# Attention and expert kernel on one core: two softmax sums, a key transpose, half the exponentials and one quarter of a transposed tile are issued at other places

## Chip, cores and metric

One Trainium2 chip, one core. The time is the device time of one execution in microseconds (us); where several runs are given, their median counts. All kernels compute the same function on the same inputs in float32.

## The reference

Three stages follow each other. `B, H, S, D = 4, 8, 512, 64`, and each of the 32 (batch, head) pairs has 32 global tokens as well.

```
s_g   = q_g @ [k_g, k_l]^T / 8           # 32 x 544, softmax, times [v_g, v_l]
s_ll  = q_l @ k_l^T / 8, masked to |i-j| <= 32
s_l   = [q_l @ k_g^T / 8, s_ll]          # softmax, times [v_g, v_l]
x     = both outputs, as 2176 used rows x 512
g     = leaky_relu(x @ w_in)             # 512 -> 2048
x     = g @ w_out                        # 2048 -> 512
out   = soft mixture of 8 experts, 4 slots each, on x (phi, w1, w2)
```

The softmax is `e / (sum(e) + 1e-9)` with the row's maximum subtracted.

## The kernel before

Local attention goes by pairs of heads. A pair is `(b, i)`, batch 0 to 3 and pair 0 to 3. For each pair the kernel has these items, and the letters are used from here on:

- **T** (`a_T`, L383): keys and queries are transposed on TensorE, four 128x128 transposes each, into a PSUM bank of the tag `tp`. ScalarE copies each out (L394, tiles `kT` and `qT`); VectorE then copies the keys' windows (L405, L406). `kT` has 4 buffers, one for each pair of a batch. T ends by issuing the loads of a later pair on SyncE's queue.
- **S** (`a_S`, L418): 64 matmuls of scores for two heads into the two banks of the tag `sc`; VectorE adds the mask and takes maxima (L446), and ScalarE makes four exponentials for each head, each with a sum (L454). VectorE then adds 1e-9 to the sums and inverts them (L459, L460).
- **E** (`a_E`, L465): the exponentials of both heads are transposed, four transposes for each head, into two `tp` banks; VectorE copies them out (L477, tile `eT`).
- **V** (`a_V`, L481): 64 matmuls with the values into the bank `po`; VectorE multiplies by the inverted sums (L501).

Each batch has global attention too: **gS** (`g_S`, L508: scores `gl` in `sc` banks, `gg` in `tp` banks, maxima, exponentials, sums and their inverse), **gE** (`g_E`, L555: two transposed heads in `tp` banks), **gG** (`g_G`: two small transposes in `tp` banks), **gV**, **gX**.

The feed-forward stage goes by 17 row tiles t of 128 rows: **X t** (`b_X`, L667: four transposes into a `tp` bank, copied out by ScalarE at L680 and then read again by VectorE at L681), **H t fq a/b** (`b_H`, L692: twelve 512-column products for quarter q in two halves of six, then a leaky ReLU on ScalarE, L717, called the Prelu), **L q t** (`b_L`, L742: quarter q of tile t transposed into a `tp` bank and copied out), **M**, **D1**, **D2**, **D3** and **U t** (`b_M`, `b_D1`, `b_D2`, `b_D3`, `b_U`: the routing logits and the running column softmax).

The tag `tp` has two PSUM banks in all, for T, E, X, L, gS, gE, gG and gX together. `hb` (for H) has two.

What sets the order: for batches 2 and 3 attention items (`step`, L640) and feed-forward items (`b_items`, L992) are merged by `merge` (L1011) in proportion to hand-written weights, and TensorE runs them in exactly that order (`manual_schedule`). The order on the other engines comes from the framework's planner, which goes by the order of the program, by what is ready in its own timeline, and by edges given with `issue_after`: an instruction in such a block stands behind the named one on its own engine. During batch 2 the row tiles 4 to 7 are worked on, during batch 3 the tiles 7 to 10.

Of the kernel before, what the change touches and what calls it, by code (L numbers as in the profile page):

```python
# [13 lines left out]
AF = mybir.ActivationFunctionType  # L14
# [6 lines left out]
def kernel(  # L21
# [393 lines left out]
    def softmax_small(mx, nmx):  # L415
        nc.vector.tensor_scalar_mul(nmx, mx, -1.0)

    def a_S(b, i):  # L418
        qt, kw = qT.pop((b, i)), kwin.pop((b, i))
        mx = sa.tile([P, 2, NT], F32, tag="mx", name="mx", bufs=2)  # L420
        nmx = sa.tile([P, 2, NT], F32, tag="nmx", name="nmx", bufs=2)
        sm = sa.tile([P, NT, 2], F32, tag="sm", name="sm", bufs=2)
        rs = sa.tile([P, NT, 2], F32, tag="rs", name="rs", bufs=2)
        es = []
        bks = [bank("sc", f"sc{e}", 2) for e in range(2)]
        if b == 0:
            for bk in bks:
                warm(bk)
        seq_ = [(T, u, e) for T in range(NT) for u in range(4) for e in range(2)]
        for T, u, e in seq_ if b > 1 else sorted(seq_, key=lambda x: x[2]):  # L430
            U = 4 * T + u
            if True:
                if True:
                    last_a[0] = nc.tensor.matmul(  # L434
                        bks[e][32 * u:32 * u + 32, P * T:P * T + P],
                        qt[64 * e:64 * e + 64, 32 * U:32 * U + 32],
                        kw[win(U) // (NW // 2)][64 * e:64 * e + 64, win(U) % (NW // 2), :],
                        start=True, stop=True,
                    ).ins
        for e in range(2):  # L440
            bk = bks[e]
            s = sa.tile([P, S + SG], F32, tag="se", name="se", bufs=4)[:, 0:S].rearrange(
                "p (t k) -> p t k", t=NT
            )
            for T in range(NT):
                nc.vector.tensor_tensor_reduce(  # L446
                    out=s[:, T, :], in0=bk[:, P * T:P * T + P],
                    in1=mask[:, 0 if T == 0 else 2 if T == NT - 1 else 1, :],
                    scale=1.0, scalar=-3.0e38, op0=ALU.add, op1=ALU.max,
                    accum_out=mx[:, e, T:T + 1],  # L450
                )
            nc.vector.tensor_scalar_mul(nmx[:, e], mx[:, e], -1.0)  # L452
            for T in range(NT):
                exp_last[0] = nc.scalar.activation(  # L454
                    out=s[:, T, :], in_=s[:, T, :], func=AF.Exp,
                    bias=nmx[:, e, T:T + 1], accum_out=sm[:, T, e:e + 1],
                ).ins
            es.append(s)
        nc.vector.tensor_scalar_add(sm, sm, 1e-9)  # L459
        nc.vector.reciprocal(rs, sm)  # L460
        sc[b, i] = (es, rs)

    eT = {}

    def a_E(b, i):  # L465
        es, rs = sc[b, i]
        ets = []
        for e in range(2):
            pt = tp("etp")
            if b == 0:  # L470
                warm(pt)
            for T in range(NT):
                last_a[0] = nc.tensor.transpose(  # L473
                    pt[:, P * T:P * T + P], es[e][:, T, :], ident
                ).ins
            et = sa.tile([P, S], F32, tag="eT", name="eT", bufs=2)
            (nc.vector.tensor_copy if b or e else nc.scalar.copy)(et, pt)  # L477
            ets.append(et)
        eT[b, i] = ets

    def a_V(b, i):  # L481
        ets = eT.pop((b, i))
        _, rs = sc.pop((b, i))
        vw = vwin.pop((b, i))
        po = bank("po", "po", 1)
        if b == 0:
            warm(po)
        pov = po.rearrange("p (t e d) -> p t e d", t=NT, e=2)
        for T in range(NT):
            for e in range(2):  # L490
                for u in range(4):
                    U = 4 * T + u
                    last_a[0] = nc.tensor.matmul(  # L493
                        pov[32 * u:32 * u + 32, T, e, :],
                        ets[e][:, 32 * U:32 * U + 32],
                        vw[:, win(U), e, :],
                        start=True, stop=True,
                    ).ins
        if i == 0:
            xn[b] = (xb[0] if b % 2 else xa).tile([P, NT, H, D], F32, tag="xn", name="xn", bufs=1)  # L500
        nc.vector.tensor_tensor(  # L501
            out=xn[b][:, :, 2 * i:2 * i + 2, :], in0=pov,
            in1=rs.unsqueeze(3).to_broadcast([P, NT, 2, D]), op=ALU.mult,
        )
# [3 lines left out]
    def g_S(b):  # L508
        mx = sa.tile([P, 2, 2], F32, tag="gmx", name="gmx", bufs=1)
        nmx = sa.tile([P, 2], F32, tag="gnmx", name="gnmx", bufs=1)  # L510
        sm = sa.tile([P, 2, 2], F32, tag="gsm", name="gsm", bufs=1)
        rs = sa.tile([P, 2], F32, tag="grs", name="grs", bufs=1)
        es = []
        for e in range(2):
            bl = bank("sc", "gl", 2)
            bg = tp("gg")
            for i in range(NP):
                lq = qgT[64 * e:64 * e + 64, i, 32 * b:32 * b + 32]
                nc.tensor.matmul(
                    bl[32 * i:32 * i + 32, :], lq, kT[b, i][64 * e:64 * e + 64, :],  # L520
                    start=True, stop=True,
                )
            for i in range(NP):
                lq = qgT[64 * e:64 * e + 64, i, 32 * b:32 * b + 32]
                nc.tensor.matmul(
                    bg[32 * i:32 * i + 32, 0:SG], lq,
                    kgT[64 * e:64 * e + 64, i, 32 * b:32 * b + 32],
                    start=True, stop=True,
                )
            nc.vector.reduce_max(out=mx[:, e, 0:1], in_=bl, axis=AX.X)  # L530
            nc.vector.reduce_max(out=mx[:, e, 1:2], in_=bg[:, 0:SG], axis=AX.X)
            nc.vector.tensor_reduce(
                out=nmx[:, e:e + 1], in_=mx[:, e], axis=AX.X, op=ALU.max, negate=True
            )
            s = sa.tile([P, S + SG], F32, tag="se", name="gs", bufs=4)
            nc.scalar.activation(
                out=s[:, 0:S].rearrange("p (t q) -> p t q", t=NT),
                in_=bl.rearrange("p (q t) -> p t q", t=NT),
                func=AF.Exp, bias=nmx[:, e:e + 1],
                accum_out=sm[:, e, 0:1],  # L540
            )
            nc.scalar.activation(  # L542
                out=s[:, S:S + SG], in_=bg[:, 0:SG], func=AF.Exp, bias=nmx[:, e:e + 1],
                accum_out=sm[:, e, 1:2],
            )
            es.append(s)
        sms = sa.tile([P, 2], F32, tag="gsms", name="gsms", bufs=1)
        nc.vector.tensor_reduce(out=sms, in_=sm, axis=AX.X, op=ALU.add)
        nc.vector.tensor_scalar_add(sms, sms, 1e-9)
        nc.vector.reciprocal(rs, sms)  # L550
        for i in range(NP):
            kT.pop((b, i))
        gst[b] = [es, rs]

    def g_E(b):  # L555
        es, rs = gst[b]
        ets = []
        for e in range(2):
# [1 line left out]
            for T in range(NT):  # L560
                nc.tensor.transpose(pt[:, P * T:P * T + P], es[e][:, P * T:P * T + P], ident)
            et = sa.tile([P, S], F32, tag="eT", name="get", bufs=2)
            nc.vector.tensor_copy(et, pt)
            ets.append([et])
            if b < 2:
                g_G(b, e, ets)
        gst[b].append(ets)

    def g_G(b, e, ets):
        es = gst[b][0]  # L570
# [64 lines left out]
    def T_(n):  # L635
        a_T(*order[n])
        if n >= NP:
            load_ahead(n + 2)

    def step(n):  # L640
# [3 lines left out]
        e = (0.9, lambda: a_E(b, i))  # L644
        v = (1.6, lambda: (a_V(b, i), None if n < NP else load_vn(b) if i == NP - 2 else load_v(n + (1 if last else 2))))
        ns = [(2.7, lambda: a_S(*order[n + 1]))] if n + 1 < NN else []
        nt = [(0.9, lambda: T_(n + 2))] if n + 2 < NN else []
        if not last:
            gs = [(2.2, lambda: g_S(b))] if i == NP - 2 else []
            return ns + [e] + gs + nt + [v]  # L650
        gv = (2.1, lambda: (g_V(b), load_v(n + 2) if b else None))
        if b < 2:
            return [e, (0, lambda: None), v, (1.1, lambda: g_E(b))] + ns + nt + [gv]
# [38 lines left out]
    def b_H(t, f, half=None):  # L692
# [21 lines left out]
            return  # L714
        gs = gt[t][:, 512 * f:512 * f + 512]
        with ahead(t):
            nc.scalar.activation(out=gs, in_=hp, func=AF.Prelu, alpha=0.01)  # L717
        if t in BLK or t in HALF and f < 2:
            blocks(t, f, gs)

# [200 lines left out]
    def l_items(t):  # L921
        return ([(0.0, lambda: None), (0.6, lambda: b_M(t, range(2)))] if t in BLK else [
            (0.6, lambda: b_M(t, range(2))) if t in HALF else (0.9, lambda: (b_L(t, 0), b_L(t, 1))),
            (0.9, lambda: (b_L(t, 2), b_L(t, 3))),
        ]) + [
            (1.3, lambda: b_D1(t)),
            (0.3, lambda: first(b_D2, t)),
# [64 lines left out]
    def b_items(t0, t1):  # L992
        its, d3, u = [], [], []
        for t in range(t0, t1):
# [6 lines left out]
            if t - 1 in BLK:  # L1001
# [1 line left out]
                its += [li[3]] + h[5:8] + [li[4]]  # L1003
                d3, u = [], [li[5]]
                continue
            its += [h[0]] + d3 + [h[1]] + u + [li[1], h[2], h[3], li[0]] + x + [h[4], li[2]]
            its += [h[5], li[3], h[6], h[7]]
            d3, u = [li[4]], [li[5]]
        return its + d3 + u
# [424 lines left out]
```

## Time and profile before

| | |
|---|---|
| median of 3 runs | 492.76 us (491.17 to 493.52) |
| the profiled execution | 490.33 us, of which span 488.6 us |
| TensorE busy (matmul) | 451.3 us, 92% of the span |
| VectorE, ScalarE, GpSimd busy | 275.7, 234.2, 160.0 us (56, 48, 33%) |
| batches 2 and 3 | about 186 to 326 us from the span's start |
| mean granted TensorE clock | 0.970 of full speed |

The span runs from the first to the last instruction in the profile; 1.73 us of the profiled execution lie outside it. A matmul counts as busy from its start to a modelled end, so that the records of consecutive matmuls overlap.

### The profile page before, as it was taken

How to read it: one execution, taken by the hardware profiler on the slowest of the kernel's cores; microseconds unless marked ns; L12 is line 12 of the kernel's file. 1: busy time of each engine (PE TensorE's matmuls, PEld its weight loads, DVE VectorE, ACT ScalarE, POOL GpSimd, SP SyncE). 2: the span in 40 equal slices, each digit the busy share in tenths (PEclk: the TensorE clock that was granted, in tenths of full speed). 3: DMA queues.
4: the chain of work that ended last, by engine and by line, in shares of the span. 5: the costliest groups of instructions: out<-in, count | busy, mean ns of one | idle time of the engine just before them, and what ended most of it. 6: DMA issues, size and time to landing. Idle time of an engine off the chain costs nothing.

```text
span 488.6 us, 13462 instructions
## 1 busy us (share of the span) xinstructions
PE 451.3 (92%) x5341; PEld 316.7 (65%) x5341; DVE 275.7 (56%) x880; ACT 234.2 (48%) x678; POOL 160.0 (33%) x281
## 2 busy tenths in 40 slices
PE   7868789998989999999999998999999999999982
PEld 5645668676766666776777775777777777743341
DVE  4685879389557676566555655535665532242223
ACT  4776799587854445444245544134443342321021
POOL 2044887433310202632335160524775530000000
PEclk9985699999999999999999999999999999999997
DMA  9989688499664575442440230279200269989997
GB/s 177 224 201 248 203 246 346 149 310 303 204 167 109 115 150 88 102 104 62 130 107 1 60 60 19 71 259 405 112 1 2 87 224 318 395 324 397 349 304 253
DMA packets 111990, 90.23 MB, mean 185 GB/s; under 512 B 75256, under 2 KB 94392, under 8 KB 111928
## 3 DMA queue, kind: packets, MB, share of 16 engines
q1 hardware_dynamic: 110024, 88.33, 61.9%
q10 hardware_dynamic: 1904, 1.05, 0.8%
q8 instruction: 42, 0.69, 0.6%
q14 instruction: 20, 0.16, 0.1%
HBM read 76.68 MB, written 8.65 MB: 175 GB/s over the span
## 4 chain that ended last, share of the span: by engine, by line
PE 74%; ACT 7%; DMA 6%; DVE 5%; SPq 4%; issue 2%; POOL 1%; DVEq 0%; ACTq 0%; POOLq 0%
PE hp L709 37%; DMA rraw<-in_moe_w_in_dram 4%; PE gtp L747 3%; PE sc L434 3%; PE ehp L1298 3%; PE up L832 3%; PE po L493 2%; PE lg L761 2%; PE etp L473 2%; PE xtp L674 1%; PE wotp L345 1%; PE sop L1332 1%; SPq L162 1%; PE gpo L585 1%; ACT se L454 1%
## 5 line engine op out<-in xcount | busy, mean ns | idle before, releaser
L709 PE MATMUL hp<-wi,xxh 128*128 128x512 f32 x512 | 168.0, 409 | 1.3 <-ACT xxh L680 1.3
L738 POOL COPY g<-gb 32x256 f32<-32x256 f32 x206 | 82.6, 401 | 87.6 <-DVE gb L729 59.1
L709 PEld LDWEIGHTS hp<-wi,xxh 128*128 128x128 f32 x512 | 92.1, 191 | 24.2 <-issue 5.3
L709 PE MATMUL hp<-wi,xxl 128*128 128x512 f32 x256 | 101.5, 397 | 0.0
L717 ACT ACTIVATE g<-hp 128x512 f32<-128x512 f32 x60 | 35.7, 594 | 78.4 <-PE hp L709 70.0
L454 ACT ACTIVATE se<-se,nmx 128x128 f32<-128x128 f32 x128 | 49.7, 390 | 19.9 <-DVE nmx L452 17.2
L709 PEld LDWEIGHTS hp<-wi,xxl 128*128 128x128 f32 x256 | 48.6, 190 | 11.7 <-issue 0.8
L200 POOL COPY vw<-vw 32x1664 f32<-32x1664 f32 x10 | 15.8, 1579 | 72.1 <-DMA vw<-in_v_g_dram 29.7
L446 DVE CUSTOM_DVE_ANT_0 se<-sc,mask 128x128 f32<-128x128 f32 x128 | 28.9, 285 | 11.8 <-PE sc L434 11.7
L261 POOL TENSOR_TENSOR wn<-wn,rraw 128x512 int32<-128x512 int32 x16 | 22.7, 1424 | 35.6 <-DVE wn L257 33.4
L729 DVE STREAM_TRANSPOSE gb<-g 128x512 f32<-128x512 f32 x32 | 22.7, 709 | 19.8 <-ACT g L717 19.6
L434 PE MATMUL sc<-kw,qT 64*32 64x128 f32 x1024 | 27.5, 283 | 0.7 <-DVE mx L446 0.4
L261 POOL TENSOR_TENSOR wo<-wo,rraw 128x512 int32<-128x512 int32 x12 | 16.0, 1332 | 31.6 <-DVE wo L257 7.2
L493 PE MATMUL po<-vw,eT 128*32 128x64 f32 x1024 | 21.9, 229 | 3.4 <-issue 2.7
L434 PEld LDWEIGHTS sc<-kw,qT 64*32 64x32 f32 x1024 | 19.7, 109 | 7.6 <-issue 4.2
L454 ACT ACTIVATION_READ_ACCUMULATOR se<-se,nmx 128x1 f32 x128 | 24.1, 189 | 0.0
L493 PEld LDWEIGHTS po<-vw,eT 128*32 128x32 f32 x1024 | 17.4, 115 | 9.4 <-issue 8.0
L473 PE MATMUL etp<-identr,se 128*128 128x128 f32 x128 | 22.5, 300 | 0.2
L477 DVE COPY eT<-etp 128x512 f32<-128x512 f32 x28 | 18.4, 682 | 6.6 <-PE etp L473 6.6
L405 DVE COPY kw<-kT 128x672 f32<-128x672 f32 x32 | 20.0, 660 | 3.6 <-ACT kT L394 3.2
L747 PE MATMUL gtp<-identr,g 128*128 128x128 f32 x112 | 16.9, 281 | 4.7 <-ACT gs L542 1.9
L251 ACT ACTIVATE rraw<-rraw 128x512 int32<-128x512 uint32 x28 | 18.8, 674 | 4.7 <-POOL wo L261 2.8
(228 smaller groups left out, 757.2 us busy)
## 6 DMA issues: line engine op xcount, KB each, us to landing
ew<-in_moe_w_dram SPq DMA_DIRECT2D x23, 1024.0 KB, 8.8
rraw<-in_moe_w_in_dram SPq DMA_DIRECT2D x16, 512.0 KB, 6.2
ew<-in_moe_w_dram SPq DMA_DIRECT2D x15, 512.0 KB, 8.9
vw<-in_v_l_dram SPq DMA_DIRECT2D x60, 112.0 KB, 3.6
rraw<-in_moe_w_out_dram SPq DMA_DIRECT2D x12, 512.0 KB, 6.5
wo_f<-wo SPq DMA_DIRECT2D x16, 256.0 KB, 4.1
vn<-in_v_l_dram SPq DMA_DIRECT2D x4, 1024.0 KB, 6.0
wo<-wo_f SPq DMA_DIRECT2D x4, 1024.0 KB, 8.0
```

Source lines behind the costliest of these rows:

```text
L261: nc.gpsimd.tensor_tensor(out=di, in0=di, in1=m, op=ALU.add)
L405: nc.vector.tensor_copy(kw[:, :, 0:96], src)
L434: last_a[0] = nc.tensor.matmul(bks[e][32 * u:32 * u + 32, P * T:P * T + P], qt[64 * e:64 * e + 64, 32 * U:32 * U + 32], kw[win(U) // (NW / ...
L446: nc.vector.tensor_tensor_reduce(out=s[:, T, :], in0=bk[:, P * T:P * T + P], in1=mask[:, 0 if T == 0 else 2 if T == NT - 1 else 1, :], sca ...
L454: exp_last[0] = nc.scalar.activation(out=s[:, T, :], in_=s[:, T, :], func=AF.Exp, bias=nmx[:, e, T:T + 1], accum_out=sm[:, T, e:e + 1],).ins
L473: last_a[0] = nc.tensor.transpose(pt[:, P * T:P * T + P], es[e][:, T, :], ident).ins
L493: last_a[0] = nc.tensor.matmul(pov[32 * u:32 * u + 32, T, e, :], ets[e][:, 32 * U:32 * U + 32], vw[:, win(U), e, :], start=True, stop=True ...
L709: nc.tensor.matmul(hp, a[:, k, :], w[c][:, k, :], start=(n == 0 and half != 1), stop=(n == len(prods) - 1 and half != 0),)
L717: nc.scalar.activation(out=gs, in_=hp, func=AF.Prelu, alpha=0.01)
L729: nc.vector.transpose(out=gb[:, f % 2], in_=gs)
L738: copy(dst[32 * c:32 * c + 32, :, a], src[32 * a:32 * a + 32, :, c])
L747: nc.tensor.transpose(pt[:, P * c:P * c + P], g[:, o:o + P], ident)
```

## The change

- **Sums.** For batches 2 and 3, the two VectorE instructions that add 1e-9 to the sums and invert them (now `a_R`) are no longer traced in S but at the end of E, behind the copy of E's second head on VectorE. The same for the three of global attention (`g_R`), behind the second copy in gE.
- **Second head.** For all pairs after (2, 0), S makes only the first head's exponentials. The second head's four are an item of their own, **S2**, queued on ScalarE behind the Prelu that was traced last. S weighs 1.7 in `merge` and S2 1.0, in place of 2.7.
- **Keys ahead.** In batch 2 the item T of (3, 0) comes before gS.
- **Fourth quarter apart.** For tiles 4 to 9, L 3 is no longer in one item with L 2; it stands behind the next half of H and adds 0.5 to the weights of each tile. L 2 keeps the weight of both, 0.9.

```diff
+    def apart(b, i):
+        return (b, i) > (2, 0)
+    def a_X(s, e, nmx, sm):
+        for T in range(NT):
+            exp_last[0] = nc.scalar.activation(
+                out=s[:, T, :], in_=s[:, T, :], func=AF.Exp,
+                bias=nmx[:, e, T:T + 1], accum_out=sm[:, T, e:e + 1],
+            ).ins
+    def a_S2(go):
+        with tc.issue_after(relu[0]):
+            go()
...
-            for T in range(NT):
-                exp_last[0] = nc.scalar.activation(...)
             es.append(s)
+            if e == 0 or not apart(b, i):
+                a_X(s, e, nmx, sm)
+        sc[b, i] = (es, (sm, rs))
+        if b < 2:
+            a_R(b, i)
+        return lambda: a_X(es[1], 1, nmx, sm)
+
+    def a_R(b, i):
+        sm, rs = sc[b, i][1]
         nc.vector.tensor_scalar_add(sm, sm, 1e-9)
         nc.vector.reciprocal(rs, sm)
...
         eT[b, i] = ets
+        if b > 1:
+            with tc.issue_after(ins):   # the copy of the second head
+                a_R(b, i)
...
+        if b > 1:                       # at the end of g_E
+            with tc.issue_after(ins):
+                g_R(b)
...
+        if ns and apart(*order[n + 1]):
+            go = []
+            ns = [(1.7, lambda: go.append(a_S(*order[n + 1]))), (1.0, lambda: a_S2(go[0]))]
...
-            return ns + [e] + gs + nt + [v]
+            return ns + [e] + (gs + nt if b < 2 else nt + gs) + [v]
...
-            nc.scalar.activation(out=gs, in_=hp, func=AF.Prelu, alpha=0.01)
+            relu[0] = nc.scalar.activation(out=gs, in_=hp, func=AF.Prelu, alpha=0.01).ins
...
-            (0.9, lambda: (b_L(t, 2), b_L(t, 3))),
+            (0.9, lambda: (b_L(t, 2), None if t in HALF else b_L(t, 3))),
...
-            its += [h[0]] + d3 + [h[1]] + u + [li[1], h[2], h[3], li[0]] + x + [h[4], li[2]]
+            its += [h[0]] + d3 + [h[1]] + u + [li[1], h[2], (0.5, lambda t=t - 1: b_L(t, 3)), h[3], li[0]] + x + [h[4], li[2]]
```

Since `merge` goes by the weights, the order of TensorE changes at other places too. Worked out from the code, with the items that write `tp` banks in brackets and H standing for one half:

```
place   before                                      after
1  H [E20] H [T22 X5] H V20                    H H [E20 X5 T22] H V20
2  H [E21] H [T23 L2 4 L3 4] H V21             H [E21 L2 4 T23] H V21 [L3 4] H
3  H U4 [E23 L2 5 L3 5] H V23 H                H V22 U4 [L2 5 E23] H V23 [L3 5] H
4  [E22] H [gS] D2 H H H [T30] V22             [E22] D2 H [T30] H [gS] H D3 H V22
5  H [gE] M [X7] S30 H                         H M [gE X7] H S30
6  H [gG] D2 [T31] H gV                        H [gG T31] H gV
7  H H [E31] M [T33 X9] H                      H [L3 7] H [E31] M [X9 T33] H
8  D3 H [gS] U7 [L2 8 L3 8] H V32 H            D3 H U7 [gS L2 8] H [L3 8] V32 H
9  M [E33 X10] H V33                           M [X10] H [E33] D1 V33
```

## Rows read from the trace of the kernel before

**Rows 1.** Busy time of each engine in three stretches; then clock, DMA share, GB/s.
```profile
190.00:258.00 68.00, 66.37 (x913) 50.25 (x912) 40.26 (x140) 30.56 (x109) 27.09 (x53) 1.00 0.40 91
258.00:326.00 68.00, 65.42 (x949) 48.46 (x948) 36.81 (x138) 29.75 (x100) 22.36 (x50) 1.00 0.23 63
326.00:395.00 69.00, 68.85 (x452) 50.84 (x453) 42.00 (x110) 29.26 (x76) 44.15 (x110) 1.00 0.35 133
```

**Rows 2.** Groups of TensorE instructions, 186 to 330 us: busy, mean ns | idle before, releasers.
```profile
L747 PE MATMUL gtp<-identr,g 128*128 128x128 f32 x48 | 7.1, 283 | 3.2 <-ACT gs L542 1.9 <-DVE eT L477 1.0 <-ACT kT L394 0.3
L674 PE MATMUL xtp<-identr,xn 128*128 128x128 f32 x28 | 4.6, 286 | 1.0 <-ACT kT L394 0.5 <-DVE eT L477 0.4
```

**Rows 3.** Waits of VectorE, 186 to 330 us: total us, times, longest.
```profile
DVE sm L459 <- ACT se L454: 3.5, 4, 2.2
```

**Rows 4.** Groups of ScalarE instructions, 186 to 330 us, columns as in rows 2.
```profile
L454 ACT ACTIVATE se<-se,nmx 128x128 f32<-128x128 f32 x56 | 21.7, 390 | 9.5 <-DVE nmx L452 6.9 <-DVE nm L785 2.6
```

**Rows 5.** Chain that ended last, 264 to 270 us: start, us, what.
```profile
264.55 0.87 PE etp L473 x8
...
265.65 1.39 PE hp L709 x6
```

**Rows 6.** Timeline, E33 and X10: start, us, what [idle before, releaser].
```profile
305.06 1.09 PE L473 MATMUL etp<-identr,se 128*128 128x128 f32 x8
...
305.85 1.25 DVE L477 COPY eT<-etp 128x512 f32<-128x512 f32 x2
...
306.56 0.66 PE L674 MATMUL xtp<-identr,xn 128*128 128x128 f32 x4 [0.41 <-DVE eT L477]
```

**Rows 7.** Timeline, T33 and X9.
```profile
280.76 0.66 PE L390 MATMUL kTp<-identr,kn 128*128 128x128 f32 x4
...
281.45 0.60 ACT L394 ACTIVATE kT<-kTp 128x512 f32<-128x512 f32 x1 [0.52 <-PE kTp L390]
...
282.10 0.66 PE L674 MATMUL xtp<-identr,xn 128*128 128x128 f32 x4 [0.24 <-ACT kT L394]
...
282.79 0.60 ACT L680 ACTIVATE xxh<-xtp 128x512 fp32r<-128x512 f32 x1 [0.26 <-PE xtp L674]
...
283.57 0.67 DVE L681 SCALAR_TENSOR_TENSOR xxl<-xtp,xxh 128x512 fp32r<-128x512 f32 x1
```

**Rows 8.** Timeline, E23, L2 5 and L3 5.
```profile
230.52 1.09 PE L473 MATMUL etp<-identr,se 128*128 128x128 f32 x8
...
232.06 0.66 PE L747 MATMUL gtp<-identr,g 128*128 128x128 f32 x4 [0.45 <-DVE eT L477]
...
233.26 0.66 PE L747 MATMUL gtp<-identr,g 128*128 128x128 f32 x4 [0.54 <-DVE eT L477]
```

**Rows 9.** Timeline, gS of batch 3, U7, L2 8 and L3 8.
```profile
295.13 1.12 PE L519 MATMUL gl<-kT,qgT 64*32 64x512 f32 x16
...
296.24 1.06 PE L832 MATMUL up<-g,d 128*32 128x512 f32 x8
296.26 0.69 DVE L530 TENSOR_REDUCE gmx<-gl 128x1 f32<-128x512 f32 x1 [0.34 <-PE gg L525]
...
298.45 0.66 PE L747 MATMUL gtp<-identr,g 128*128 128x128 f32 x4 [1.15 <-ACT gs L542]
...
299.88 0.66 PE L747 MATMUL gtp<-identr,g 128*128 128x128 f32 x4 [0.77 <-ACT gs L542]
```

**Rows 10.** Timeline, gE of batch 2 and X7, then gG and T31.
```profile
237.77 1.03 PE L561 MATMUL get<-identr,gs 128*128 128x128 f32 x8
...
238.74 0.65 PE L761 MATMUL lg<-g,pmat 128*32 128x128 f32 x16
...
239.02 0.70 DVE L729 STREAM_TRANSPOSE gb<-g 128x512 f32<-128x512 f32 x1
...
244.64 0.38 PE L572 MATMUL geg<-identr,gs 128*32 128x128 f32 x2
...
245.28 0.66 PE L390 MATMUL kTp<-identr,kn 128*128 128x128 f32 x4
```

More of the change, by code (lines that the diff above doesn't have):

```diff
@@ L416, in softmax_small @@
         nc.vector.tensor_scalar_mul(nmx, mx, -1.0)
+    def apart(b, i):
+        return (b, i) > (2, 0)
+    relu = [None]
+    def a_X(s, e, nmx, sm):
[7 more added lines that the diff above has]
+            go()
     def a_S(b, i):
@@ L452, in a_S @@
             nc.vector.tensor_scalar_mul(nmx[:, e], mx[:, e], -1.0)
-            for T in range(NT):
[L454 to L457, printed above, removed]
-            es.append(s)
+            es.append(s)
+            if e == 0 or not apart(b, i):
[6 more added lines that the diff above has]
+        sm, rs = sc[b, i][1]
         nc.vector.tensor_scalar_add(sm, sm, 1e-9)
         nc.vector.reciprocal(rs, sm)
-        sc[b, i] = (es, rs)
     eT = {}
@@ L476, in a_E @@
             et = sa.tile([P, S], F32, tag="eT", name="eT", bufs=2)
-            (nc.vector.tensor_copy if b or e else nc.scalar.copy)(et, pt)
+            ins = (nc.vector.tensor_copy if b or e else nc.scalar.copy)(et, pt).ins
             ets.append(et)
         eT[b, i] = ets
+        if b > 1:
+            with tc.issue_after(ins):
+                a_R(b, i)
     def a_V(b, i):
         ets = eT.pop((b, i))
-        _, rs = sc.pop((b, i))
+        rs = sc.pop((b, i))[1][1]
         vw = vwin.pop((b, i))
@@ L546, in g_S, with g_R @@
             es.append(s)
+        gst[b] = [es, rs]
+        gst["sm"] = sm
+        if b < 2:
+            g_R(b)
+        for i in range(NP):
+            kT.pop((b, i))
+    def g_R(b):
+        sm, rs = gst.pop("sm"), gst[b][1]
         sms = sa.tile([P, 2], F32, tag="gsms", name="gsms", bufs=1)
@@ L550, in g_S @@
         nc.vector.reciprocal(rs, sms)
-        for i in range(NP):
-            kT.pop((b, i))
-        gst[b] = [es, rs]
     def g_E(b):
@@ L562, in g_E @@
             et = sa.tile([P, S], F32, tag="eT", name="get", bufs=2)
-            nc.vector.tensor_copy(et, pt)
+            ins = nc.vector.tensor_copy(et, pt).ins
             ets.append([et])
@@ L567, in g_E @@
         gst[b].append(ets)
+        if b > 1:
+            with tc.issue_after(ins):
+                g_R(b)
     def g_G(b, e, ets):
```

## The prediction

> **What bounds the kernel now.** I read the busy times by stage first. In the two stretches that hold batches 2 and 3 TensorE is busy 66.4 and 65.4 of 68 us, VectorE and ScalarE about half, and the clock is full (1.00) [rows 1]. After them it is busy 68.85 of 69 us: what this change could bring has to come out of batches 2 and 3, and it is at most what TensorE idles there. The groups of TensorE instructions say where that is: 3.2 us before the transposes of L and 1.0 us before those of X, nothing anywhere else, each time until an engine has copied out a `tp` bank [rows 2]. So the whole prize is the turnover of two banks.
>
> How long such a turnover takes is in the timelines. Eight transposes of E are issued in 0.87 us, so one bank's four take 0.44, and half an H covers 1.39 us [rows 5]. From the first transpose of E to the moment when TensorE may write that bank again it takes 306.56 - 305.06 = 1.50 us; VectorE began 0.79 after the transposes did, though the first bank was full at about 0.63 (0.44 issued and a tail of about 0.2), so 1.34 when VectorE is free. The two copies last 1.25 us together, so the second bank comes 0.6 us after the first, at 1.94 [rows 6]. A bank of T takes 282.10 - 280.76 = 1.34 as well; a bank of X goes through ScalarE and then VectorE, which ends 284.24 - 282.10 = 2.1 us after X begins [rows 7]. I count a wait from the end of the issue before it, which is about 0.2 us longer than the idle time in the view, because the last matmul's record runs on.
>
> So counted, the waits of before are: X5 behind T22 0.47, L2 4 behind T23 0.46, X9 behind T33 0.45 (one pattern, thrice; the last of them is in [rows 7]: 282.10 - 280.76 - 0.87 = 0.47, less what T itself lost); L2 5 and L3 5 behind E23 232.06 - 230.52 - 0.87 = 0.67 and 233.26 - 232.06 - 0.44 = 0.76 [rows 8]; L2 8 and L3 8 behind gS 1.2 and 1.0 [rows 9]; X10 behind E33 306.56 - 305.06 - 0.87 = 0.63 [rows 6]. Sum 5.7 us (4.2 by the view's idle time, and eight times 0.2).
>
> **Part by part: sums.** VectorE waits 3.5 us in four places for exponentials before it can treat a sum [rows 3]. No wait in [rows 2] has VectorE's L459 or L460 in it: what stands behind them is late for nobody. Moved, they cost the same two instructions for each pair, in front of the next copy at worst, some 0.4 us. I take 0; below, nothing too, since no row names them.
>
> **Second head.** 56 exponentials lie in the stretch, 390 ns each, so the eight of a pair are 3.1 us of ScalarE [rows 4]; S2 halves the block that a Prelu or a copy of `kT` may stand behind. Of the waits in [rows 2], those for `kT` are 0.8 us together, and there ScalarE had been idle before the copy (0.52 us in [rows 7]): the exponentials were not what it waited for. I take 0. Their E comes a whole step later, so S2 is not late either. What S2 can hit is a copy of L that now falls due while it runs: a block of four is 1.6 us. I take 0 here and keep 0.7 us for the range (the part of it that half an H, 1.39 us, does not cover, with the copy itself).
>
> **The order on TensorE.** This is where I expect the difference: the new weights move which users of `tp` follow each other without H between them (places 1 to 9 of the list in the section on the change). Bank times are from the paragraph above, from the first transpose of the cluster.
>
> 1. E20, X5, T22 are five banks in a row, where H stood between. X5 waits until 1.34 (0.47 lost), T's keys until 1.94 (0.16 lost), T's queries until the keys' bank is back at 1.94 + 1.34 = 3.28, where TensorE is ready at 2.38: 0.90. Sum 1.53, before 0.47.
> 2. E21, L2 4, T23: 0.47, then 0.16, then L2's bank, one copy on ScalarE like T's, back at 1.34 + 1.34 = 2.68 against 2.38: 0.30. Sum 0.93, before 0.46.
> 3. L2 5 in front of E23 and L3 5 behind half an H and V: only E's second head waits, for L2's bank, 1.34 - 0.88 = 0.46. Before 1.43. This is what setting the fourth quarter apart brings.
> 4. T30 in front of gS: `kT` has four buffers, and pairs (2, 0) to (2, 3) hold them until gS has read the keys. So the copy of the new keys can't start before gS's matmuls are done, and its bank is withheld from gS's own `gg`. The trace of before has no such wait. Below, 0.5 us (the copy alone, if it starts while gS is being issued), above 1.3 (both `tp` copies behind each other after it). I take 0.7, nearest to the copy of [rows 7], 0.65 from its start to the next transposes.
> 5. gE and X7 without M between: 1.34 - 0.87 = 0.47, and the block transpose of g, 0.70 us, falls due just there [rows 10]. I take 0.6, before 0.
> 6. gG and T31 without D2 between: the bank is back 245.28 - 244.64 = 0.64 us after gG begins, and gG itself fills 0.38 of it [rows 10]. 0.26, before 0.04.
> 7. M (0.65 us with its tail, some 0.6 issued [rows 10]) covers X9 behind E31, but T33 is now behind X9: its queries need the keys' bank, 1.34 later, with 0.44 issued: 0.90. Before 0.45.
> 8. L2 8 directly behind gS. Its bank waits for maxima and exponentials and came back 298.45 - 295.13 = 3.32 us after gS began [rows 9]. U7 no longer fills 1.0 of it; L2 loses 3.32 - 1.1 = 2.2, L3 behind half an H nothing. Before 1.2 + 1.0 = 2.2: no gain where most idle time is.
> 9. X10 behind half an H is free (before 0.63), but V33 now has only D1 (as many matmuls as M) between E33 and itself and needs both copies, at 1.94: 1.94 - 0.87 - 0.6, so 0.47.
>
> Sum after 8.0 us, before 5.7: +2.3 us. On SyncE's queue T30's loads move with it, but gS issues none, so they pass nothing there; a pair's loads are wanted two steps later, and no row of TensorE in [rows 2] waits for a load. GpSimd's queue keeps its order.
>
> **One rule against this.** The sum needs TensorE not to run H's matmuls past transposes that wait. [Rows 2] show idle time before `gtp` while H's operands lay ready, so it did not. The Trainium skill, page "TensorE: Matmul & The Clock Gate", section "Step-by-step: what each phase is for", says that matmuls stay in program order and only weight loads are pulled ahead; by that rule the whole +2.3 us is paid; if matmuls could pass, neither the waits of before nor the new ones would count, and the time would stay at 492.8.
>
> **Rivals.** (a) *The places cancel* (nothing changes): the new clusters cost only the first wait of 0.47 each, since copies that overlap better than in [rows 6, 7] refill the second bank in time. Then 1, 2 and 7 fall by 1.9 us, and 0.4 is left: 493.2. For it: VectorE and ScalarE are half idle [rows 1]. Against: the second and third waits are chains of one copy each, whoever is idle.
> (b) *ScalarE and VectorE collide with the copies* (slower): at place 7 L3 7 comes right behind S2, and its copy waits for four exponentials (0.7 us); at places 1 and 5 the block transpose of g (0.70) goes in front of the second copy, 0.6 each more. 2.3 + 1.9 = +4.2: 497.0. It decides from where the planner puts the Prelu's follow-up in front of `eT`, as it did in [rows 8], where the second copy came 1.2 us after the first.
> (c) *The turnover is shorter throughout* (faster): if the waits of before came from late copies rather than from the turnover itself, sums and exponentials out of the way would start every copy at once; then 3, 8 and 9 go to 0 as well and places 1, 2 and 7 to 0.47 each: 1.4 + 1.6 for 4 to 6 less 5.7 = -2.7, 490.1. Against it: in [rows 6, 7] the copy starts within 0.1 to 0.2 us of the last transpose. It decides from waits of L2 8 under 0.5 us.
>
> **The numbers.** The profiled execution has 490.33 us, its span 488.6; the sum gives 492.6 for such a one. The median of the runs shown is 2.4 above the profiled execution, and a measured time is a median too: 492.76 + 2.3 = 495.0 us, +0.47%. A measurement of this kernel tells a change from none at about 0.5%, 2.46 us. Chances: the sum as it stands 52%, its own range 493.3 to 497.3 (place 4 between 0.5 and 1.3, places 1 and 5 up to 0.6 more each, place 9 between 0 and 0.6); this lies across the bound, 33% within it and 19% above. (a) 13%, within. (b) 18%, slower. (c) 17%, faster. So faster 0.17, same 0.46, slower 0.37. For eight in ten the range goes from half way to (c), 491.0, to somewhat above (b), 498.0.
>
> **What would show it.** In the trace after: waits of the kind `kTp <- DVE xxl` or `qTp <- ACT kT` at places 1 and 7, which before has none of; `gg` waiting for `kT` at place 4; L2 8 waiting some 2 us for `gs`; no wait of L3. TensorE's idle time over batches 2 and 3 should rise from 4.2 to about 6 us, and VectorE's wait at the sums should be gone without a gain. I am wrong if idle time falls, if H runs between the members of a cluster, or if the difference lies outside batches 2 and 3.

## The result, and the profile after

| | before | after |
|---|---|---|
| median | 492.40 us (491.17 to 493.52, 4 runs) | 498.81 us (497.42 to 500.87, 4 runs) |
| profiled execution, span | 490.33, 488.6 us | 499.29, 497.6 us |
| from U 3 to U 10 | 184.33 to 350.33: 166.0 us | 185.40 to 358.93: 173.5 us |

The change makes the kernel slower: ratio 1.0134, 95% interval 1.009 to 1.0179. The third row of the table goes from the first matmul `up<-g,d` of row tile 3 to that of row tile 10, which is all of batches 2 and 3 as far as TensorE's order differs. I call it the stretch: it grew by 7.5 us. The rest of the span is 1.5 us longer in this pair of profiles, 1.1 ahead of the stretch and 0.4 behind it. That is scatter: the stretch starts anywhere between 183.1 and 188.2 us in the profiles of this study (at 185.4 and 183.5 in two of the changed kernel itself), so that stretches are better compared than single spans.

After the change the lines have other numbers: E is L492 (copy L496), H L743, L L781 (copy L783), X L708, V L515 (multiplication L523), U L866, gS L541 to L564.

The busy times of the engines in three stretches answer [rows 1], with the same columns:

```profile
190.00:258.00 68.00, 62.24 (x884) 46.77 (x883) 39.83 (x147) 29.88 (x105) 25.51 (x52) 1.00 0.36 82
258.00:326.00 68.00, 64.09 (x925) 48.20 (x924) 37.04 (x139) 28.51 (x97) 23.95 (x51) 0.97 0.21 49
326.00:395.00 69.00, 68.85 (x470) 50.64 (x471) 38.40 (x101) 27.14 (x68) 36.36 (x92) 1.00 0.38 139
```

TensorE is busy 4.1 us less in the first and 1.3 in the second than before, the same in the third, and in the second the clock is no longer full (matmuls at a lower clock count as busy). TensorE's waits after, 186 to 334 us (waited for, releaser: total us, times, longest):

```profile
PE gtp L781 <- ACT gs L564: 2.9, 1, 2.9
PE qTp L390 <- ACT kT L394: 2.1, 3, 0.7
PE etp L492 <- DVE eT L496: 1.0, 1, 1.0
PE up L866 <- DVE xn L523: 0.8, 1, 0.8
PE gg L547 <- ACT kT L394: 0.8, 1, 0.8
PE kTp L390 <- DVE geg L605: 0.6, 1, 0.6
PE xtp L708 <- DVE get L591: 0.4, 1, 0.4
...
```

With three more of 0.3 us each (X, L and V, all for E's copy) they sum to 9.5 us, against 4.2 in [rows 2]. All but one (`up`, below) are for a `tp` bank or its copy. VectorE's 3.5 us at the sums [rows 3] are gone from its waits; what that was worth is told with the first experiment.

Place 2 on the timeline (E21, L2 4, T23):

```profile
208.56 1.03 PE L492 MATMUL etp<-identr,se 128*128 128x128 f32 x8
...
209.94 0.66 PE L781 MATMUL gtp<-identr,g 128*128 128x128 f32 x4 [0.35 <-DVE eT L496]
...
210.54 0.66 PE L390 MATMUL kTp<-identr,kn 128*128 128x128 f32 x4
211.23 0.60 ACT L394 ACTIVATE kT<-kTp 128x512 f32<-128x512 f32 x1 [1.06 <-PE kTp L390]
211.72 0.58 ACT L783 COPY gT<-gtp 128x512 f32<-128x512 f32 x1
211.88 0.66 PE L390 MATMUL qTp<-identr,qn 128*128 128x128 f32 x4 [0.69 <-ACT kT L394]
```

ScalarE copied the keys before L 2, which had been transposed 0.6 us earlier, and the queries took the keys' bank, 211.88 - 210.54 = 1.34 us after the keys began in it. The turnover of [rows 7] again, to a hundredth, but of the other bank than I had said. Place 3 (end of V22, U4, L2 5, E23):

```profile
232.59 1.10 PE L515 MATMUL po<-vw,eT 128*32 128x64 f32 x64
233.75 0.69 DVE L523 TENSOR_TENSOR xn<-po,rs 128x512 f32<-128x512 f32 x1
234.50 1.07 PE L866 MATMUL up<-g,d 128*32 128x512 f32 x8 [0.81 <-DVE xn L523]
235.50 0.66 PE L781 MATMUL gtp<-identr,g 128*128 128x128 f32 x4
...
235.99 0.60 PE L492 MATMUL etp<-identr,se 128*128 128x128 f32 x4
236.24 0.59 ACT L783 COPY gT<-gtp 128x512 f32<-128x512 f32 x1
...
236.93 0.65 DVE L496 COPY eT<-etp 128x512 f32<-128x512 f32 x1
237.63 0.66 PE L492 MATMUL etp<-identr,se 128*128 128x128 f32 x4 [1.05 <-DVE eT L496]
```

Two things. U 4 waits 0.81 us for V's result to be read out: V and U share one PSUM bank (`po` and `up`), and the new order sets U 4 directly behind V22, where half an H and a D3 stood between. And E's second head did not take L's bank, free at 236.83, but that of its own first head, free at 237.58. Place 8 (U7, gS, L2 8), VectorE and ScalarE between:

```profile
302.52 1.12 PE L541 MATMUL gl<-kT,qgT 64*32 64x512 f32 x16
302.66 0.75 DVE L873 SCALAR_TENSOR_TENSOR uacc<-uacc,al,up 128x512 f32<-128x512 f32 x1 [0.26 <-PE up L866]
303.36 0.71 DVE L763 STREAM_TRANSPOSE gb<-g 128x512 f32<-128x512 f32 x1
304.00 0.65 DVE L552 TENSOR_REDUCE gmx<-gl 128x1 f32<-128x512 f32 x1
...
304.67 0.67 DVE L552 TENSOR_REDUCE gmx<-gl 128x1 f32<-128x512 f32 x1
305.27 0.13 DVE L554 TENSOR_REDUCE gnmx<-gmx 128x1 f32<-128x2 f32 x1
...
306.62 0.66 PE L781 MATMUL gtp<-identr,g 128*128 128x128 f32 x4 [2.92 <-ACT gs L564]
```

The bank comes back 306.62 - 302.52 = 4.10 us after gS began, not 3.32 as in [rows 9]. Two things on VectorE make up the 0.78. gS's maxima now stand behind U 7's sum and a block transpose and begin 1.48 us after gS, in place of 1.13. And the second head's 512-wide maximum (304.67) now stands in front of the step that the first head's exponentials wait for (305.27), so that from the first maximum to the first exponential it takes 1.52 us, in place of 1.09. And this is the granted clock (the number before the DMA share) in the two-microsecond windows behind the wait:

```profile
306.00:308.00 2.00, 1.39 (x8) 1.26 (x9) 0.00 (x0) 1.98 (x9) 0.00 (x0) 0.96 0.00 0
308.00:310.00 2.00, 2.00 (x7) 1.32 (x6) 0.00 (x0) 0.00 (x0) 0.00 (x0) 0.50 0.04 8
310.00:312.00 2.00, 2.00 (x67) 1.83 (x67) 0.24 (x1) 0.58 (x1) 0.00 (x0) 0.69 0.00 0
```

0.50 is the lower of the two levels, 1.2 GHz. From L 2 to the end of V32, 306.62 to 311.61, the work takes 4.99 us; at full clock it takes 3.44 (measured below), so 1.5 us went there.

### The profile page after: what moved, and what is told of

The parts are those of the page before. It is cut to its first block, busy times and chain, and to the rows that moved or that the text cites. A ratio compares the mean times of both kernels' runs of the same rounds, so it can differ in the third digit from the quotient of the medians.

```text
span 497.6 us, 13463 instructions
## 1 busy us (share of the span) xinstructions
PE 454.1 (91%) x5341; PEld 318.5 (64%) x5341; DVE 276.3 (56%) x880; ACT 235.3 (47%) x678; POOL 159.0 (32%) x281
## 4 chain that ended last, share of the span: by engine, by line
PE 72%; DVE 7%; ACT 4%; DMA 3%; issue 1%; POOL 0%; DVEq 0%; SPq 0%; ACTq 0%; POOLq 0%
PE hp L743 37%; PE gtp L781 4%; PE sc L450 3%; PE ehp L1332 3%; PE up L866 3%; PE po L515 2%; PE lg L795 2%; PE etp L492 2%; DMA ew<-in_moe_w_dram 2%; PE xtp L708 1%; PE wotp L345 1%; PE sop L1366 1%; PE gpo L616 1%; PE qTp L390 1%; PE ptps L354 1%
## 5 line engine op out<-in xcount | busy, mean ns | idle before, releaser
L743 PE MATMUL hp<-wi,xxh 128*128 128x512 f32 x512 | 167.5, 409 | 1.1 <-ACT xxh L714 1.1
L743 PEld LDWEIGHTS hp<-wi,xxh 128*128 128x128 f32 x512 | 91.3, 190 | 23.0 <-issue 5.1
L743 PE MATMUL hp<-wi,xxl 128*128 128x512 f32 x256 | 101.8, 398 | 0.4 <-DVE xxl L715 0.4
L743 PEld LDWEIGHTS hp<-wi,xxl 128*128 128x128 f32 x256 | 48.6, 190 | 12.6 <-DVE xxl L715 1.0
L515 PE MATMUL po<-vw,eT 128*32 128x64 f32 x1024 | 22.3, 231 | 3.7 <-issue 2.0
L496 DVE COPY eT<-etp 128x512 f32<-128x512 f32 x28 | 18.5, 685 | 12.8 <-PE etp L492 12.8
L515 PEld LDWEIGHTS po<-vw,eT 128*32 128x32 f32 x1024 | 17.7, 116 | 9.6 <-issue 6.6
L492 PE MATMUL etp<-identr,se 128*128 128x128 f32 x128 | 22.6, 300 | 1.3 <-DVE eT L496 1.0
L781 PE MATMUL gtp<-identr,g 128*128 128x128 f32 x112 | 17.9, 286 | 4.6 <-ACT gs L564 2.9
L523 DVE TENSOR_TENSOR xn<-po,rs 128x512 f32<-128x512 f32 x16 | 11.0, 688 | 18.9 <-PE po L515 17.9
```

Of the source, the lines that this page charges most:

```text
L492: last_a[0] = nc.tensor.transpose(pt[:, P * T:P * T + P], es[e][:, T, :], ident).ins
L515: last_a[0] = nc.tensor.matmul(pov[32 * u:32 * u + 32, T, e, :], ets[e][:, 32 * U:32 * U + 32], vw[:, win(U), e, :], start=True, stop=True ...
L743: nc.tensor.matmul(hp, a[:, k, :], w[c][:, k, :], start=(n == 0 and half != 1), stop=(n == len(prods) - 1 and half != 0),)
L781: nc.tensor.transpose(pt[:, P * c:P * c + P], g[:, o:o + P], ident)
```

## The experiments

The kernel before ran again beside each group of kernels, with medians of 491.49, 491.16 and 491.11 us, and each ratio is to the runs beside it. Across groups the ratios are to be compared rather than the times; the changed kernel has 1.0134, and 1.0153 when it ran again.

Most kernels move items in the list that `merge` makes, in this way (source and target position in the list, one move after the other):

```diff
-    def merge(a, c):
+    def merge(a, c, moves=()):
...
-            f()
+            fs.append(f)
+        for src, dst in moves:
+            fs.insert(dst, fs.pop(src))
+        for f in fs:
+            f()
```

**The two halves of the change.** *order_only*: the changed kernel's order on TensorE, with the sums and all eight exponentials where they were.

```diff
-            if e == 0 or not apart(b, i):
-                a_X(s, e, nmx, sm)
+            a_X(s, e, nmx, sm)
-        if b < 2:
-            a_R(b, i)
-        return lambda: a_X(es[1], 1, nmx, sm)
+        a_R(b, i)
+        return lambda: None
```

(g_R likewise.)

> TensorE's order is exactly that of the changed kernel (498.8 us); the second head's exponentials and all sums are back where the kernel before has them. If the order over the two transpose banks is the whole loss: within 1.5 us of 498.8. If the moved exponentials and sums are the loss, because they come in front of copies on ScalarE and VectorE: back to 492.4, within 1.5.

*parts_only*: the old order, with the sums and the second head's exponentials moved.

```diff
-            ns = [(1.7, lambda: go.append(a_S(*order[n + 1]))), (1.0, lambda: a_S2(go[0]))]
+            ns = [(2.7, lambda: go.append(a_S(*order[n + 1]))), (0.0, lambda: a_S2(go[0]))]
-            return ns + [e] + (gs + nt if b < 2 else nt + gs) + [v]
+            return ns + [e] + gs + nt + [v]
-            (0.9, lambda: (b_L(t, 2), None if t in HALF else b_L(t, 3))),
+            (0.9, lambda: (b_L(t, 2), b_L(t, 3))),
```

(and the item L 3 taken out of the list.)

> The other half: TensorE's order is exactly that of the kernel before (492.4 us), the sums stand behind the copies and the second head's exponentials behind the Prelu as in the changed kernel (the item for them has no weight, and L 2, L 3, T and gS are where they were). If the order is the whole loss: 492.4, within 1 us. If the moved exponentials and sums cost: 495 to 499. If they gain what the change hoped for and the order hid it: 490 or less.

Measured: order_only 497.95 us, ratio 1.0118 (1.0075 to 1.0162), with the changed kernel's waits, 2.9 for `gs` and three times 0.7 for `kT` among them. parts_only 491.95 us, ratio 1.0007 (0.9979 to 1.0034). The order on TensorE is the whole difference that the times show; sums and exponentials are worth nothing measurable.

The profile of order_only has one wait that the changed kernel has not, 0.7 us at place 1, where T22's keys wait for E20's second copy:

```profile
195.64 0.17 DVE L477 TENSOR_SCALAR sm<-sm 128x8 f32<-128x8 f32 x1 [0.55 <-ACT se L425]
195.72 0.68 DVE L494 COPY eT<-etp 128x512 f32<-128x512 f32 x1
```

There VectorE waits for exponentials at a sum (L477 in this kernel), and E's copy (L494) stands behind it. So under the new order the moved sums spare a wait of 0.7 us, of a kind that before had none of; the times don't show it.

**The half clock.** *clock_fill*: twelve matmuls into an `hb` bank behind gS of batch 3; their result is not used.

```diff
+        if b == B - 1:
+            wm = hb("wm")
+            for _ in range(12):
+                warm(wm)
```

> The changed kernel, with 12 extra 128x512 matmuls of the identity into a free bank behind the last global scores, where TensorE stood idle for 2.9 us and then ran at half clock. The wait for the bank stays, only the idleness goes. If the half clock behind the wait costs what its slow groups show (0.6 + 0.4 + 0.5 = 1.5 us): 497.3, and half an H there lasts 1.39 in place of 1.98 us. If the clock fell for another reason, or the slow stretch is hidden: 498.8.

Measured: 498.02 us, ratio 1.0109 (1.0063 to 1.0154). The windows of this kernel over the same place:

```profile
304.00:308.00 4.00, 4.00 (x41) 3.04 (x26) 2.35 (x8) 1.79 (x8) 0.00 (x0) 1.00 0.00 0
308.00:312.00 4.00, 4.00 (x79) 3.24 (x79) 0.69 (x1) 1.26 (x4) 0.00 (x0) 1.00 0.02 5
```

The clock stays full, L 2 to V32 takes 3.44 us in place of 4.99, and the stretch is 1.5 us shorter (172.0). In the time there is less, 0.8 us (1.2 by the ratios) with intervals that overlap, so the times don't show a gain. The other profiles give a likely reason: order_only idles the same 2.9 us at this place and keeps its full clock (L 2 to V32 in 3.45 us), while parts_only, with waits of 1.15 and 0.77 us there, falls to 0.68 behind them (300 to 304 us). So the 1.5 us need not be lost in every execution; in how many they are, these runs don't tell.

**Place 8 by itself.** *gs_apart*: in batch 3, half an H and V32 between gS and L2 8.

```diff
+        merge(attn[b - 1], head[:-6], {2: [], 3: [(41, 44), (42, 45)]}[b])
```

> The changed kernel with two items of batch 3 moved: behind the last global scores come half an H and V32, then L2 8, half an H and L3 8. Nothing else moves. If the wait of L2 8 on the banks of the global scores is real loss (3.0 us) and the half clock its consequence (1.5): 494.3. If only the wait goes and the clock falls anyway: 495.8. If TensorE loses the same time at the next place: 498.8.

Measured: 495.24 us, ratio 1.0073 (1.0046 to 1.0099). L's wait for `gs` is 0.3 us, the clock full, the stretch 170.6. The time lies between the first two expectations: by the ratios 3.0 us are gained of 4.5. A wait is new: E31's transposes, 0.9 us, for L3 7's copy, which here stands behind late exponentials on ScalarE. The moves did not bring it, since the changed kernel shows it too when it runs again (below). It is where rival (b) had its place 7.

**Three clusters broken up.** *three_broken*: at places 1, 2 and 7 half an H (and a V) between the members.

```diff
+        merge(attn[b - 1], head[:-6], {2: [(9, 7), (8, 10), (8, 8), (21, 19), (21, 20), (21, 22)], 3: [(25, 26)]}[b])
```

> The changed kernel, with H or V put back between the members of its three clusters of five transpose groups (places 1, 2 and 7). Measured from the trace these cost 1.56, 1.56 and 1.0 us there. If a cluster's wait is paid in full: 498.8 - 4.1 = 494.7, ratio to before 1.005. If the waits merely pass to the next users: 498.8.

Measured: 496.87 us, ratio 1.0124 (1.0091 to 1.0157), by the time in the middle of the two expectations. By the ratio it is not: 1.005 was expected if the waits are paid, which lies outside the interval, and a gain against the changed kernel's 1.0134 is not shown. The profile has one all the same, a stretch of 170.6. Its trace has no wait left at the three places, and from U 3 to U 4, which holds places 1 and 2, the time is 3.3 us shorter (45.8 for 49.1), from U 4 to U 7 0.9. But behind gS the half clock lasted longer than in the changed kernel:

```profile
304.00:308.00 4.00, 2.79 (x9) 2.40 (x10) 0.24 (x2) 2.58 (x9) 0.00 (x0) 0.55 0.02 4
308.00:312.00 4.00, 4.00 (x73) 3.19 (x72) 0.43 (x1) 0.59 (x1) 0.00 (x0) 0.59 0.00 0
```

L 2 to V32 took 305.21 to 311.42, 6.2 us: 2.8 lost where the changed kernel lost 1.5. So in this profile the 4.1 us are there, 3.0 in the stretch and 1.3 that the clock took back; for the four times that is not shown.

**V apart from U.** *v_apart*: V22 ahead, so that U 4 doesn't follow it, and T30 behind gS.

```diff
+        merge(attn[b - 1], head[:-6], {2: [(41, 39), (35, 41)], 3: []}[b])
```

> The changed kernel with two items moved in batch 2: V22 in front of D3 and half an H, so that U4 no longer follows it directly (both write the one bank of the tag po), and T30 behind gS again. If the 0.8 us that U4 waits for V's copy and the 0.8 us that gg waits for the keys are real: 1.9 us less with their tails, 496.9. If not: 498.8.

Measured: 497.74 us, ratio 1.0145 (1.0116 to 1.0173): nothing gained, stretch 173.5. Both waits are gone from the trace, 0.8 for `xn` and 0.8 for `kT`; in their place E23's second head waits 1.5 in place of 1.0, and at E31 stands a new one:

```profile
279.98 0.60 PE L781 MATMUL gtp<-identr,g 128*128 128x128 f32 x4
...
281.34 0.56 ACT L783 COPY gT<-gtp 128x512 f32<-128x512 f32 x1
...
281.95 0.66 PE L492 MATMUL etp<-identr,se 128*128 128x128 f32 x4
...
283.39 0.66 PE L492 MATMUL etp<-identr,se 128*128 128x128 f32 x4 [0.78 <-DVE eT L496]
```

These transposes are L3 7 and then the two heads of E31. ScalarE makes its two copies for tile 7 only at 281.34 and 283.36, each behind four exponentials, though L2 7's transposes had begun at 278.11; in the changed kernel its first copy followed them at once (282.17 behind 281.43). So both banks are held: E31's first head starts when the first copy is done, and the second 1.44 us later, when the first's bank is back. The order on ScalarE is the planner's, which put the copy elsewhere when two items on TensorE had moved. A turnover that was taken out came back at another place in this way; it is one case and no rule.

**The repairs together.** Three kernels on one chip: the changed kernel again, three_broken with gs_apart (*broken_apart*), and both with v_apart (*all_apart*).

```diff
+        # broken_apart; all_apart has (41, 39), (35, 41) as well in 2
+        merge(attn[b - 1], head[:-6], {2: [(9, 7), (8, 10), (8, 8), (21, 19), (21, 20), (21, 22)], 3: [(25, 26), (41, 44), (42, 45)]}[b])
```

> The changed kernel itself, once more, on the chip on which the next two run. 498.8 us (497.4 to 500.9) as before, with 2.9 us of TensorE's wait for L 2 of tile 8 and half the clock behind it. How long the half clock lasts is what I want to see a second time: 1.5 us were lost to it in the first profile of this kernel, 2.8 in that of the kernel with three clusters broken up.

> The changed kernel with both repairs at once: the clusters at places 1, 2 and 7 broken up, and gS of batch 3 kept apart from L 2 of tile 8. Theory (the clusters' waits are paid in full, and with the clusters broken up alone the difference went into a longer half clock): with no wait of 2.9 us there is no half clock, so that the waits of the clusters, 4.1 us, come off the 495.2 of the kernel with gS apart: 491.1 us, TensorE's clock full throughout. Rival (the waits of the clusters are in part passed on to waits behind them, so that breaking them up is worth only the 1.9 us measured before): 493.3 us.

> As the kernel before it, and pair (2, 2)'s V moved ahead, so that U 4 no longer stands directly behind it, with the transposes of (3, 0) behind gS of batch 2. Theory (U 4's wait of 0.8 us for the shared bank and gg's of 0.8 us for the keys are paid, and in the kernel that moved V alone they were given back, 0.5 us at E of (2, 3) and 0.8 us at E of (3, 1), which there stood behind a late copy of L 3 of tile 7): 1.1 us below the kernel before it, 490.0, if E of (3, 1) does not wait; 490.8 if it does. Rival (they are passed on whatever stands behind them): as the kernel before it.

Measured: after_again 498.34 us, ratio 1.0153 (1.0111 to 1.0195); broken_apart 491.31, ratio 0.9998 (0.9972 to 1.0023); all_apart 490.50, ratio 0.999 (0.996 to 1.0019). broken_apart came out where the first theory had it, 491.1, and not at the rival's 493.3. Against gs_apart it is 3.7 us faster by the ratios (1.9 to 5.5 with both intervals, which has the rival's 1.9 at its edge), and its stretch is 5.4 us shorter (165.2), about 1.1 of it E31's wait. Its waits:

```profile
PE etp L492 <- DVE eT L496: 1.0, 1, 1.0
PE up L866 <- DVE xn L523: 0.8, 1, 0.8
PE gg L547 <- ACT kT L394: 0.8, 1, 0.8
PE kTp L390 <- DVE geg L605: 0.7, 1, 0.7
...
```

With three more of 0.3 to 0.4 us they sum to 4.3 us, as many as before has, and the time is that of before. all_apart trades again: the two waits of 0.8 are out, E23 (0.5 more) and E31 (0.8) wait in their place; the 0.8 us between the two medians lie within the measurement. In after_again the half clock cost 1.5 us a second time, and the stretch is 174.9. E31 also waits 0.9 us for L3 7's copy, which it did not in the first profile of the same code. The trace shows why:

```profile
281.07 1.58 POOL L200 COPY vw<-vw 32x1664 f32<-32x1664 f32 x1 [9.63 <-DMA vw<-in_v_g_dram]
281.12 1.56 DVE L468 TENSOR_SCALAR nmx<-mx 128x4 f32<-128x4 f32 x1
...
284.27 0.56 ACT L783 COPY gT<-gtp 128x512 f32<-128x512 f32 x1
...
284.88 0.66 PE L492 MATMUL etp<-identr,se 128*128 128x128 f32 x4 [0.94 <-ACT gT L783]
```

GpSimd copies values when their load has landed. Here it starts just ahead of the step that the first head's exponentials wait for (L468), which takes 1.56 us in place of 0.16 (last section); the four exponentials come late by as much, and L3 7's copy behind them. In gs_apart it is the same, with 1.50. In the first profile of the changed kernel GpSimd began after that step (283.45 against 282.89), and the copy was back in time.

**Before with its own waits taken out.** *six_moves*: the kernel before, none of the change, with six items moved behind the next half of H, or behind V: X5, X9, X10 and the pairs L 2, L 3 of tiles 4, 5 and 8.

```diff
+        merge(attn[b - 1], head[:-6], {2: [(7, 8), (18, 19), (40, 41)], 3: [(22, 23), (37, 39), (43, 44)]}[b])
```

> The kernel before, with none of the change, and six items of TensorE's order moved so that half an H or more stands wherever its trace shows a wait for a transpose bank: X5, L2 and L3 of 4 and of 5, X9, L2 and L3 of 8 (behind half an H and V32), X10. If the turnover of the two banks is all that TensorE loses in batches 2 and 3: the 5.7 us of before go, ratio 0.989 (about 486 where before has 491.5), and no wait for a bank is left in the trace. If the waits come back at the next users, or the loss lies elsewhere: 0.996 to 1.0.

*six_moves_parts*: the same order, in parts_only (sums and second head moved as in the change).

> The same order of TensorE as the kernel with six moves, with the sums behind the copies and the second head's exponentials as items of their own in addition. If these two never stood in the way: the same time as with the six moves alone, within 1 us. If they gain once the banks are no longer what is waited for: 1 to 2 us less. If they collide with copies: 1 to 2 us more.

Measured: six_moves 485.67 us (485.04 to 486.19), ratio 0.9888 (0.9864 to 0.9912); six_moves_parts 484.64, ratio 0.9887 (0.9844 to 0.993). Both beat both kernels. TensorE in six_moves, in the two stretches of [rows 1]:

```profile
190.00:258.00 68.00, 67.96 (x952) 52.25 (x958) 41.58 (x153) 31.64 (x111) 27.18 (x53) 1.00 0.42 92
258.00:326.00 68.00, 68.00 (x965) 51.42 (x949) 39.96 (x144) 30.25 (x101) 26.02 (x59) 1.00 0.31 91
```

Busy throughout; the stretch is 160.4 us, 5.6 below before. The 5.7 us that I had counted as before's waits were all of them to be had, by order alone. With sums and exponentials moved as well the ratio is the same.

## Why the prediction was wrong

The mechanism held, and the sizes did not: TensorE does not pass a waiting transpose, the waits for two `tp` banks are paid, and the weights' side effect on the order (not the sums, not the exponentials) decides. H's matmuls show no idle time of their own (0.0 us before L743, 186 to 334 us), yet none filled the waits and the stretch grew. That agrees with the Trainium skill, page "TensorE: Matmul & The Clock Gate", section "Step-by-step: what each phase is for", by which matmuls stay in program order. Forecast +2.3 us, measured +6.4 in the medians and +7.5 in the stretch, beyond even rival (b). The steps that failed are the times at which I had banks come back at places 8 and 3 (3.0 and 1.2 us lost for 2.2 and 0.46), a clock that I took to stay full behind place 8 (1.5), and a path left out, the bank that V and U share (1.0). The terms, counted as in the prediction:

| place | before | predicted after | measured after |
|---|---|---|---|
| 1 | 0.47 | 1.53 | 1.57 |
| 2 | 0.46 | 0.93 | 1.57 |
| 3 | 1.43 | 0.46 | 1.2, and U 4 1.0 |
| 4 | 0 | 0.7 | 0.95 |
| 5 | 0 | 0.6 | 0.63 |
| 6 | 0.04 | 0.26 | 0.63 |
| 7 | 0.45 | 0.90 | 0.95 |
| 8 | 2.2 | 2.2 | 3.0, and the clock 1.5 |
| 9 | 0.63 | 0.47 | 0.4 |
| sum | 5.7 | 8.0 | 11.9 + 1.5 |

13.4 less 5.7 is 7.7, against 7.5 in the stretch.

- **Places 1, 4, 5, 7 and 9** came out as costed, within 0.25 us. **Sums and second head**: 0, as said (parts_only).
- **Place 8 is the largest miss, 2.3 us.** I took 3.32 us for the bank's return from [rows 9], where U 7 stood behind gS. With U 7 ahead, its sum on VectorE (0.75) and the Prelu's follow-up (0.71) stand in front of gS's maxima (0.35 later), the second head's maximum stands in front of the first head's exponentials (0.43 more), and 0.8 is lost. I had counted what U 7 no longer fills, and not what it now delays. Joined into one, the idle time was followed by half the clock in this profile (1.5 us), which I had not reckoned with; order_only shows that it need not be.
- **Place 3, 1.7 us.** "Only E's second head waits, for L2's bank": it waited for the first head's. I took the bank that comes free first; the trace shows the other taken. With L's bank, free at 236.83, the wait would have been 236.83 - 236.43 = 0.40, about what I had. Why the other was given out is open: no experiment tried the choice of bank by itself. And I followed only the `tp` banks: V22 directly ahead of U 4 stood in my own list, but that V and U share a bank I had not looked up.
- **Place 2, 0.6 us.** The same step as place 3: queries in the keys' bank, not in L's, and ScalarE copies the keys first.
- **Place 6, 0.4 us.** VectorE was held up by GpSimd, see the last section.
- **Rivals.** (a) and (c) are out: nothing cancelled, and the turnover was 1.34 us wherever it was not held up. (b) was right in kind and not in its places: VectorE's follow-ups stood in front of a copy or of gS's maxima at places 3 and 8, at place 5 they cost 0.16 us more than a bare turnover and at place 1 nothing, and at place 7 the 0.9 us came in two profiles, behind GpSimd. With 4.2 it would still have been too low.
- **The range.** From the terms that the prediction names, the sum's own range is 494.3 to 496.9 us (497.6 with the 0.7 kept for S2), and not 493.3 to 497.3. The measured time is above either, and above the 498.0 of the whole range.

## What to carry to other kernels

When weights of a merged order change, list who uses each PSUM bank directly behind whom, for every tag and not just the busiest: what costs here is two users of the same bank without other matmuls between. Price a turnover with everything that the new order puts in front of its copy on the copying engine, and don't presume which bank the next tile gets; read it from the trace or from the planner. Six moves by one or two places gave 1.1%, the finer-grained scheduling of two other engines nothing.

## What the runs showed of the hardware

**Small VectorE instructions beside a GpSimd copy.** At place 6 (GpSimd, VectorE, TensorE, VectorE):

```profile
250.61 1.57 POOL L200 COPY vw<-vw 32x1664 f32<-32x1664 f32 x1
...
250.76 1.44 DVE L819 TENSOR_TENSOR nm<-nm 128x1 f32<-128x1 f32 x1
...
251.62 0.38 PE L603 MATMUL geg<-identr,gs 128*32 128x128 f32 x2
...
252.31 0.47 DVE L605 COPY geg<-geg 32x128 f32<-32x128 f32 x2
```

A minimum over one element in each partition takes 1.44 us (0.16 at the median) and ends with GpSimd's copy, so that `geg`'s copy comes late: the transposes of T31 begin 252.63 - 251.62 = 1.01 us after `geg`'s, 0.64 in [rows 10]. In all nine profiles of kernels that have the changed order at this place the minimum takes 1.44 to 1.52 us there; in before, parts_only and six_moves it comes behind `geg`'s copy, and T31 begins after 0.64. In this profile it happened to L819 again at 224.79 (1.27 us, the copy from 224.47) and to L468 at 283.59 (1.47, from 283.45). The Trainium skill, page "SBUF — State Buffer", section "SBUF: two separate sides", states that VectorE and GpSimd share one pair of ports under an exclusive lock, which VectorE wants for an instruction with two operands in SBUF or in a two-port mode, and that the loser waits for the whole instruction. The two ends, 252.20 and 252.18 us, agree with it. L468 has one operand in SBUF, and whether it runs in a two-port mode no run here shows. Not every small instruction is held up: the inverse of the sums (L480, 128x8) took its usual 0.19 us at 224.67, beside the copy from 224.47.

**The clock behind a wait.** The granted clock fell from 1.00 to 0.50 at a wait of 2.9 us, in its last microsecond or within 1.3 us behind it, in four profiles (after, after_again, three_broken, v_apart) and not in order_only with the same wait; it fell behind two shorter ones in parts_only, and not in before with the same two. It cost 1.5 us each time but once, 2.8.
